# Weight sums and most low parts of the second product by GpSimd alone, and 56 fewer, wider stores of weight blocks

## The chip, the cores and the metric

The kernel runs on one core of one Trainium2 chip. The metric is the device time of one launch in microseconds; the median over runs is what counts. Engines: TensorE (PE, with weight loads as PEld), VectorE (DVE), ScalarE (ACT), GpSimd (POOL), SyncE (SP). Each works through its own queue in order. SP computes nothing here: nearly all DMAs are issued from its queue.

## The reference

An attention over 8 batches of 8 heads (576 positions, 64 wide), heads 0 to 3 with a local mask of 32 positions, heads 4 to 7 with a mask that keeps every 32nd position, followed by a two-layer network on its 4608 x 512 result:

```python
mask_local = (rel >= 0) & (rel < stride)
mask_strided = (rel >= 0) & (pos[None, :] % stride == pos[:, None] % stride)
masks = np.stack([mask_local if h < H // 2 else mask_strided for h in range(H)], axis=0)
scores = np.where(masks[None, :, :, :], scores, -1000000000.0)
...
attn_out = np.matmul(attn, v)
x = np.ascontiguousarray(attn_out.transpose(0, 2, 1, 3)).reshape(B * S, H * D)
h = x @ w_in                                  # [4608,512] @ [512,2048]
g = h * np.clip(h + 3.0, 0.0, 6.0) / 6.0
out = g @ w_out                               # [4608,2048] @ [2048,512]
```

All in float32.

## The kernel before

**Precision.** A float32 product is made of three matmuls of a faster type: high by high, high by low, low by high. Each operand therefore has a high part (a rounding copy by ACT, "hi") and a low part (value minus high part, a subtraction by DVE or POOL, "lo").

**Stages.** Batches 0, 1 and 2 go through both products in a plain way, 512 tokens at a time (`ffn`). From about 345 us on the other five batches go in pairs, (3,4), (5,6) and (7 alone), and use sums of blocks in place of some of the products (a Strassen scheme, 7 products for 8). The pair (3,4) (`super_tile`, about 345 to 545 us) does so in the first product only; the pair (5,6) and batch 7 (`fast_tile`, about 545 to 716 and 716 to 873 us) in both. The attention of later batches is worked in between.

**Weight sums.** The scheme needs sums of weight blocks, split in high and low, in SBUF or in DRAM:

- `combine(g, k)`, eight times while batches 1 and 2 run: of two blocks of w_in it makes two sums of 128x512 (`whole`, L995), four of 128x256 (`sums`, L1003), two high parts (ACT, L1007) and two low parts (`lo`, L1011), and stores them to DRAM (L1018, tiles dS).
- `combine_out(n, slots)`, eight times while the pair (3,4) runs: the same for w_out (`whole` L1144, `sums` L1150, `lo` L1160, stores L1165, tiles dT). Its inputs are the slots `or`, into which blocks of w_out are loaded from DRAM at L1195 (or<-do); the plain second product of this stage reads the same slots.
- `keep_plain` and `keep_block` store the plain blocks (tiles dA, do).

`load_in` (L1105, wr<-dA, wr<-dS) and the loads L1417 (or<-dT) and L1426 (or<-do) in `fast_tile` bring them back.

**First and second product.** Of the first product's seven sums, P, several are gathered by DVE (`added`, L1134) and ACT (`copied`, L1129) into G; the gate is L769 (ACT) and L772 (DVE, G or u from P). L783 and L787 are the high and low parts of the gate for the plain second product (gh on ACT, gl on POOL), L1357 and L1361 (`split`) those of the fast one. `form` makes the first product's operands B (L1058 their low parts, L1064 sums). L526 transposes keys and queries for the attention (kplain, qplain), whose scores are L593. In the fast tiles L1459 adds the second product's cP into C.

**Order.** The program's order is planned when it is built. Every step is given to `op(engine, cost, function, reads, writes, due, ...)`, and `emit` plays the engines through with these costs, choosing what can start soonest, then what is due first. A step that names two engines goes to the one that is free first in this play:

```python
op({"DVE": 1.3, "POOL": 1.45}, 0, whole, reads=[slots[i]], writes=[uk[i]] + ..., due=due)
```

So costs set both the order on each engine and, for such steps, the engine. On the chip an engine runs its queue in that order and waits with whatever stands first.

Of the kernel before, what the change touches and what calls it, by code (L numbers as in the profile page):

```python
# [19 lines left out]
P = 128  # L20
# [9 lines left out]
TOK = 512  # L30
# [143 lines left out]
def attention_ffn(ctx: ExitStack, tc, q, k, v, w_in, w_out, out):  # L174
# [258 lines left out]
    def pair(g):  # L433
# [37 lines left out]
        for x in "qk":  # L471
# [47 lines left out]
            def tr(x=x, nkey=nkey):  # L519
# [6 lines left out]
                nc.vector.transpose(to, tiles[nkey])  # L526
            op("SP", 2.8, load, writes=[nkey], due=due - 35, early=due - 45, after=2.0)
            op("DVE", 0.8 if loc else 1.25, tr, reads=[nkey, "plain"], writes=[tkey[x]], due=due - 18, early=max(due - AHEAD, T0 + OPEN), room=LATE)
# [251 lines left out]
    def split_ops(gk, src, key, du, name, tail=False):  # L780

        def hi():
            nc.scalar.copy(new(xp if gk[0][0] == "x" else gp, gk[0], [P, TOK], F32R, f"gh{name}"), src())  # L783

        def lo():
            to = new(xp if gk[1][0] == "x" else gp, gk[1], [P, TOK], F32R, f"gl{name}")
            (nc.vector if tail else nc.gpsimd).tensor_tensor(out=to, in0=src(), in1=tiles[gk[0]].bitcast(F32), op=ALU.subtract)  # L787
# [157 lines left out]
    for g_ in range(NQ):  # L945
        for nm_ in ("A11", "A12", "S2", "S3", "S1", "A22", "S4"):
            scratch[nm_, g_] = drp.tile([P, 2, 2, SIDE], F32, tag=f"d{nm_}{g_}", name=f"d{nm_}{g_}")
        for nm_ in ("T1", "T2", "T3", "T4"):
            scratch[nm_, g_] = drp.tile([P, 2, 2, SIDE], F32, tag=f"d{nm_}{g_}", name=f"d{nm_}{g_}")
    for fc_ in range(NFC):  # L950
        scratch["o", fc_] = drp.tile([P, 2, TOK], F32, tag=f"do{fc_}", name=f"do{fc_}")

    def keep_block(nm, g, k, due):

        c = (EVEN if nm in ("A11", "S2", "S3") else ODD)[k]
        side = 1 if nm in ("S3", "S1", "A22") else 0
        key = wkey("i", g, c)

        def store():
            nc.sync.dma_start(scratch[nm, g][:, k], tiles[key].bitcast(F32)[:, :, SIDE * side:SIDE * side + SIDE])  # L960
        op("SP", 0.53, store, reads=[key, key + ("lo",)], writes=[("d", nm, g, k)], due=due, early=due - 4.0, after=0.8)

    def keep_plain():
        at = start[1] + 2.0
        step = (start[2] + 10.0 - at) / 24
        for g in range(NQ):
            for nm in ("A11", "A12", "A22"):
                for k in range(2):
                    keep_block(nm, g, k, at)
                    at += step  # L970
        for fc in range(NFC):
            key = wkey("o", fc // FQ, fc % FQ)
            due = start[1] + 20.0 + 6.0 * fc

            def store(fc=fc, key=key):
                nc.sync.dma_start(scratch["o", fc], tiles[key].bitcast(F32))
            op("SP", 0.53, store, reads=[key, key + ("lo",)], writes=[("d", "o", fc)], due=due, early=due - 4.0, after=1.4)

    def combine(g, k, due):
# [12 lines left out]
        for i in range(2):  # L992
            def whole(e, i=i):
                t = tiles[kw[i]].bitcast(F32)
                on(e).tensor_tensor(out=make(i, F32, f"E{g}{k}{i}"), in0=t[:, 0], in1=t[:, 1], op=ALU.add)  # L995
            op({"DVE": 1.2, "POOL": 1.35}, 0, whole, reads=[kw[i], kw[i] + ("lo",)], writes=[keys[i]] + (old(keys[0][:2], 0) if late else []), due=due)
        for n_ in range(4):
            def sums(e, n_=n_):
                u, v_ = temp(0), temp(1)
                u0, u1, v0, v1 = u[:, :SIDE], u[:, SIDE:], v_[:, :SIDE], v_[:, SIDE:]  # L1000
                o, x, y, how = ((v1, u1, v1, ALU.add), (u1, u0, u1, ALU.subtract),
                                (u0, v1, u0, ALU.subtract), (v0, v0, u0, ALU.subtract))[n_]
                on(e).tensor_tensor(out=o, in0=x, in1=y, op=how)  # L1003
# [133 lines left out]
    def combine_out(n, slots, due):  # L1137
# [3 lines left out]
        for i in range(2):  # L1141
            def whole(e, i=i):
                t = tiles[slots[i]].bitcast(F32)
                on(e).tensor_tensor(out=(u, v_)[i](), in0=t[:, 0], in1=t[:, 1], op=ALU.add)  # L1144
            op({"DVE": 1.3, "POOL": 1.45}, 0, whole, reads=[slots[i]], writes=[uk[i]] + (old(("sp", 0), 0) if not n else []), due=due)
        for m in range(4):
            def sums(e, m=m):
                u0, u1, v0, v1 = u()[:, :SIDE], u()[:, SIDE:], v_()[:, :SIDE], v_()[:, SIDE:]
                o, x, y = ((u0, u1, u0), (u1, v1, u1), (v1, v1, u0), (v0, v0, v1))[m]
                on(e).tensor_tensor(out=o, in0=x, in1=y, op=ALU.subtract)  # L1150
            op({"DVE": 0.9, "POOL": 0.85}, 0, sums, writes=uk, due=due + 0.2 + 0.1 * m)
        for i in range(2):
# [8 lines left out]
            op("ACT", 0.63, hi, reads=[uk[i]], writes=[keys[0]] + (old(("sp", 1 + i), 0) if not n else []), due=due + 0.7)  # L1161
            op({"DVE": 1.25, "POOL": 1.4}, 0, lo, reads=[uk[i], keys[0]], writes=[keys[1]], due=due + 0.8)
            for x, nm in enumerate((("T1", "T3"), ("T4", "T2"))[i]):
                def store(i=i, x=x, nm=nm):
                    nc.sync.dma_start(scratch[nm, n // 2][:, n % 2], tiles["sp", 1 + i].bitcast(F32)[:, :, SIDE * x:SIDE * x + SIDE])  # L1165
                op("SP", 0.53, store, reads=keys, writes=[("d", nm, n // 2, n % 2)], due=due + 3.0, after=0.8)

# [119 lines left out]
    def fast_tile(si):  # L1287
# [84 lines left out]
        def second_of(s):  # L1372
# [5 lines left out]
            for j, nm in enumerate(SECONDS):  # L1378
                due = w0 + 2 * j * long
                gks = []  # L1380
                for q in range(2):
# [5 lines left out]
                    if nm == "P6":  # L1387
# [27 lines left out]
                if tn:  # L1415
                    def load(wk=wk, tn=tn):
                        nc.sync.dma_start(home(wk).bitcast(F32), scratch[tn, s].rearrange("p q h d -> p q (h d)"))  # L1417
                    op("SP", 0.53, load, reads=[("d", tn, s, q) for q in range(2)], writes=[wk], due=due - 8.0, early=due - 40.0, after=1.4)
                else:
# [166 lines left out]
```

## Time and profile before

| | |
|---|---|
| median of 3 runs | 881.37 us (880.92 to 884.89) |
| the profiled execution | 884.25 us, of it the span 882.5 us |
| granted TensorE clock, mean | 0.992 of full speed |
| instructions on DVE, POOL, SP | 961, 543 rows busy on DVE and POOL; 598 DMAs or groups of them on SP |
| chain that ended last | PE 79%, POOL 5%, DMA 5%, DVE 4% |
| DMA | 179.12 MB, mean 203 GB/s; HBM written 40.89 MB |

The profile shows one execution. "Busy" is the time in which an engine worked on an instruction; a number in brackets at the end of an instruction's row is how long its engine stood idle before it and what ended that wait. The longest waits of DVE and POOL for one another, and the whole chain, in the page's words:

```profile
PE 79%; POOL 5%; DMA 5%; DVE 4%; issue 3%; ACT 2%; SPq 1%; ACTq 0%; DVEq 0%; POOLq 0%
```

It is to be read as: of the chain that led to the last instruction, four fifths were PE's own work.

### The profile page before, as it was taken

The numbers are of one execution on the slowest core, as the hardware profiler recorded it, in microseconds if no ns is written. First come the engines' busy times: TensorE is split into PE (matmuls) and PEld (weight loads), VectorE is DVE, ScalarE is ACT, GpSimd is POOL, SyncE is SP. The second block draws the span as 40 slices with busy tenths as digits, with TensorE's granted clock in tenths as the row PEclk, the third lists the DMA queues.
The fourth block names the chain that finished last, engine by engine and source line by source line (L and its number), as shares of the span: only waits on it lengthen the run. The fifth ranks groups of instructions, "written<-read, shape, count | busy, mean of one in ns | idle before, by whom it ended". The sixth has DMA issues, their size and how long they took to land.

```text
span 882.5 us, 19109 instructions
## 1 busy us (share of the span) xinstructions
PE 850.9 (96%) x6962; PEld 684.3 (78%) x6962; DVE 605.8 (69%) x961; ACT 558.1 (63%) x1246; POOL 555.3 (63%) x543
## 2 busy tenths in 40 slices
PE   8889999999999999999999799999999999999995
PEld 6667778788888888878778588788888778888884
DVE  5688868565556658683765757377777988777685
ACT  3687656777687876787677476577654645454441
POOL 4678876455547769763574687445865887545472
PEclk9999999999999999999999999999999999999999
DMA  8958713889884466799989697877666658876537
GB/s 218 316 115 230 241 32 76 208 268 246 271 241 104 121 164 196 210 245 245 263 230 266 224 303 213 222 210 207 192 187 192 194 145 250 203 238 191 179 122 141
DMA packets 342252, 179.12 MB, mean 203 GB/s; under 512 B 200784, under 2 KB 322384, under 8 KB 342160
## 3 DMA queue, kind: packets, MB, share of 16 engines
q1 hardware_dynamic: 333764, 176.35, 71.5%
q10 hardware_dynamic: 8396, 1.57, 1.0%
q8 instruction: 55, 0.90, 0.4%
q14 instruction: 37, 0.30, 0.1%
HBM read 136.97 MB, written 40.89 MB: 202 GB/s over the span
## 4 chain that ended last, share of the span: by engine, by line
PE 79%; POOL 5%; DMA 5%; DVE 4%; issue 3%; ACT 2%; SPq 1%; ACTq 0%; DVEq 0%; POOLq 0%
PE P L1122 8%; PE P L1124 7%; PE P L1123 7%; PE ph L848 5%; PE acc L825 5%; PE cP L1443 5%; PE cP L1442 5%; PE cP L1441 5%; PE acc L827 5%; PE ph L849 4%; PE ph L850 4%; PE acc L826 4%; PE acc L1208 3%; PE acc L1210 3%; PE acc L1209 3%
## 5 line engine op out<-in xcount | busy, mean ns | idle before, releaser
L787 POOL TENSOR_TENSOR gl<-u,gh 128x512 fp32r<-128x512 f32 x48 | 65.6, 1368 | 56.2 <-ACT gh L783 40.8
L1459 DVE SCALAR_TENSOR_TENSOR C<-cP,C 128x512 f32<-128x512 f32 x96 | 65.5, 686 | 25.7 <-PE cP L1443 24.9
L1122 PE MATMUL P<-B_T,wr 128*128 128x512 f32 x192 | 76.2, 397 | 3.6 <-ACT G L1129 2.0
L825 PE MATMUL acc<-wo,gh 128*128 128x512 f32 x192 | 77.0, 401 | 0.0
L827 PE MATMUL acc<-wo,gl 128*128 128x512 f32 x192 | 75.3, 392 | 0.3 <-POOL gl L787 0.2
L826 PE MATMUL acc<-wo,gh 128*128 128x512 f32 x192 | 74.9, 390 | 0.0
L1124 PE MATMUL P<-B_T,wr 128*128 128x512 f32 x192 | 74.8, 390 | 0.0
L1123 PE MATMUL P<-B_T,wr 128*128 128x512 f32 x192 | 74.8, 390 | 0.0
L1134 DVE TENSOR_TENSOR G<-P,G 128x512 f32<-128x512 f32 x64 | 43.8, 686 | 42.9 <-PE P L1124 38.3
L1129 ACT COPY G<-P 128x512 f32<-128x512 f32 x64 | 37.6, 587 | 46.5 <-PE P L1124 46.3
L658 POOL TENSOR_TENSOR e<-e,st 96x384 f32<-96x384 f32 (+1 forms) x64 | 47.1, 741 | 19.6 <-DVE st L654 19.3
L693 ACT COPY atloc<-e 32x192 f32<-32x192 f32 x144 | 50.9, 353 | 12.9 <-DVE e L683 11.4
L772 DVE SCALAR_TENSOR_TENSOR u<-u,ph 128x512 f32<-128x512 f32 x48 | 32.8, 686 | 36.3 <-ACT u L769 35.9
L1361 POOL TENSOR_TENSOR sp<-G,sp 128x512 fp32r<-128x512 f32 x26 | 36.0, 1393 | 30.0 <-ACT sp L1357 28.6
L848 PE MATMUL ph<-x,wi 128*128 128x512 f32 x128 | 52.4, 410 | 2.2 <-ACT x L419 1.1
L769 ACT ACTIVATE u<-ph,three 128x512 f32<-128x512 f32 x48 | 33.0, 688 | 31.5 <-PE ph L850 31.2
L849 PE MATMUL ph<-x,wi 128*128 128x512 f32 x128 | 50.7, 396 | 2.3 <-DVE x L422 1.6
L1122 PE MATMUL P<-B_B,wr 128*128 128x512 f32 x120 | 48.0, 400 | 4.9 <-DVE G L1134 3.3
L850 PE MATMUL ph<-x,wi 128*128 128x512 f32 x128 | 50.7, 396 | 0.0
L1123 PE MATMUL P<-B_B,wr 128*128 128x512 f32 x120 | 46.9, 390 | 0.0
L1124 PE MATMUL P<-B_B,wr 128*128 128x512 f32 x120 | 46.8, 390 | 0.0
L1122 PEld LDWEIGHTS P<-B_T,wr 128*128 128x128 f32 x192 | 36.0, 188 | 13.7 <-ACT G L1129 3.3
(619 smaller groups left out, 2673.1 us busy)
## 6 DMA issues: line engine op xcount, KB each, us to landing
wr<-dS SPq DMA_DIRECT2D x96, 256.0 KB
wr<-dA SPq DMA_DIRECT2D x72, 256.0 KB
or<-do SPq DMA_DIRECT2D x32, 512.0 KB
or<-dT SPq DMA_DIRECT2D x32, 512.0 KB
or<-do SPq DMA_DIRECT2D x48, 256.0 KB
rawi<-in_moe_w_in_dram SPq DMA_DIRECT2D x16, 512.0 KB
rawo<-in_moe_w_out_dram SPq DMA_DIRECT2D x16, 512.0 KB
do<-wo SPq DMA_DIRECT2D x16, 512.0 KB
```

Of the source, the lines that this page charges most:

```text
L693: nc.scalar.copy(at[PAD * (a + h):PAD * (a + h) + PAD, :, rows], e[rows, :, PAD * h:PAD * h + PAD])
L787: (nc.vector if tail else nc.gpsimd).tensor_tensor(out=to, in0=src(), in1=tiles[gk[0]].bitcast(F32), op=ALU.subtract)
L825: nc.tensor.matmul(acc, gh, woh, start=fc == 0, stop=False)
L826: nc.tensor.matmul(acc, gh, wol, start=False, stop=False)
L827: nc.tensor.matmul(acc, gl, woh, start=False, stop=end)
L848: nc.tensor.matmul(ph, wih, xh, start=n_ == 0, stop=False)
L849: nc.tensor.matmul(ph, wih, xl, start=False, stop=False)
L850: nc.tensor.matmul(ph, wil, xh, start=False, stop=n_ == NCC - 1)
L1122: nc.tensor.matmul(ph, wh, xh, start=fresh and k == 0, stop=False, skip_group_check=not fresh)
L1123: nc.tensor.matmul(ph, wh, xl, start=False, stop=False, skip_group_check=not fresh)
L1124: nc.tensor.matmul(ph, wl, xh, start=False, stop=k == 1, skip_group_check=not fresh)
L1459: nc.vector.scalar_tensor_tensor(out=tiles[ck], in0=tiles[bank], scalar=1.0 / 6.0, in1=tiles[ck], op0=ALU.mult, op1=ALU.add)
```

## The change

- `whole`, `sums` and `lo` of `combine` and `combine_out` name POOL alone, with costs of 1.3, 0.82 and 1.3.
- The low part in `split` names POOL alone while s is at most 1 in the pair (5,6) and at most 2 in batch 7 (s counts the four groups of the second product); after that it names both engines as before.
- Blocks that were stored side by side go out together: `combine` 32 stores of 256 KB for 64 of 128 KB, `combine_out` 16 of 512 KB for 32 of 256 KB, `keep_plain` 16 of its w_in stores for 24. The bytes stay the same. The DRAM tiles are laid out anew: A1, A2, Su, Sv, Tu, Tv, with `KEPT` saying where each block lies. A store of T is now one run of 4 KB per partition; a load of T (L1417 before) reads four runs of 1 KB per partition where it read one of 4 KB.
- Two planning costs are altered: 3.4 for 2.8 at the loads of queries and keys of batches 5 to 7, 1.3 for 1.35 at L789.

```diff
-    op("SP", 2.8, load, writes=[nkey], due=due - 35, early=due - 45, after=2.0)
+    op("SP", 3.4 if b > 4 else 2.8, load, writes=[nkey], due=due - 35, early=due - 45, after=2.0)
...
-    op("DVE" if tail else "POOL", 0.8 if tail else 1.35, lo, reads=[key, gk[0]], writes=[gk[1]], due=du)
+    op("DVE" if tail else "POOL", 0.8 if tail else 1.3, lo, reads=[key, gk[0]], writes=[gk[1]], due=du)
...
+    KEPT = {"A11": ("A1", 0), "A12": ("A2", 0), "A22": ("A2", 1), "S2": ("Su", 0), "S3": ("Su", 1), "S4": ("Sv", 0), "S1": ("Sv", 1),
+            "T1": ("Tu", 0), "T3": ("Tu", 1), "T4": ("Tv", 0), "T2": ("Tv", 1)}
...
     # combine
-            op({"DVE": 1.2, "POOL": 1.35}, 0, whole, ...)
+            op("POOL", 1.3, partial(whole, "POOL"), ...)
-            op({"DVE": 0.9, "POOL": 0.9}, 0, sums, ...)
+            op("POOL", 0.82, partial(sums, "POOL"), ...)
-            op({"DVE": 1.4, "POOL": 1.4}, 0, lo, ...)
-            for x, nm in enumerate((("S2", "S3"), ("S4", "S1"))[i]):
-                for h in range(2):
-                        nc.sync.dma_start(scratch[nm, g][:, k, h], part.bitcast(F32)[:, SIDE * x:SIDE * x + SIDE])
+            op("POOL", 1.3, partial(lo, "POOL"), ...)
+            for h in range(2):
+                    nc.sync.dma_start(scratch["Su" if i == 0 else "Sv", g][:, k, h], part.bitcast(F32))
...
     # combine_out
-            op({"DVE": 1.3, "POOL": 1.45}, 0, whole, ...)
+            op("POOL", 1.3, partial(whole, "POOL"), ...)
-            op({"DVE": 0.9, "POOL": 0.85}, 0, sums, ...)
+            op("POOL", 0.82, partial(sums, "POOL"), ...)
-            op({"DVE": 1.25, "POOL": 1.4}, 0, lo, ...)
-            for x, nm in enumerate((("T1", "T3"), ("T4", "T2"))[i]):
-                    nc.sync.dma_start(scratch[nm, n // 2][:, n % 2], tiles["sp", 1 + i].bitcast(F32)[:, :, SIDE * x:SIDE * x + SIDE])
-                op("SP", 0.53, store, reads=keys, writes=[("d", nm, n // 2, n % 2)], due=due + 3.0, after=0.8)
+            op("POOL", 1.3, partial(lo, "POOL"), ...)
+                nc.sync.dma_start(scratch[("Tu", "Tv")[i], n // 2][:, n % 2], tiles["sp", 1 + i].bitcast(F32))
+            op("SP", 0.53, store, reads=keys, writes=[("d", ("Tu", "Tv")[i], n // 2, n % 2)], due=due + 3.0, after=1.4)
...
     # split
-            op({"DVE": 1.25, "POOL": 1.4}, 0, lo, reads=[key, gk[0]], writes=[gk[1]], due=du)
+            if both:
+                op({"DVE": 1.25, "POOL": 1.4}, 0, lo, reads=[key, gk[0]], writes=[gk[1]], due=du)
+            else:
+                op("POOL", 1.3, partial(lo, "POOL"), reads=[key, gk[0]], writes=[gk[1]], due=du)
...
     # the loads of T in fast_tile
-                        nc.sync.dma_start(home(wk).bitcast(F32), scratch[tn, s].rearrange("p q h d -> p q (h d)"))
+                        at, x = KEPT[tn]
+                        nc.sync.dma_start(home(wk).bitcast(F32).rearrange("p q (h d) -> p (q h) d", h=2),
+                                          scratch[at, s][:, :, :, SIDE * x:SIDE * x + SIDE].rearrange("p q h d -> p (q h) d"))
```

How many instructions each line has on the two engines, before and after (after's line numbers are a few off; before's are given):

| line | what | DVE | POOL |
|---|---|---|---|
| L995, L1003, L1011 | combine: whole, sums, lo | 6, 13, 8 to 0 | 10, 19, 8 to 16, 32, 16 |
| L1144, L1150, L1160 | combine_out: whole, sums, lo | 6, 10, 4 to 0 | 10, 22, 12 to 16, 32, 16 |
| L1361 | second product's low parts | 41 to 14 | 71 to 98 |
| L1058, L1064 | form: low parts, sums of operands | 18, 9 to 22, 11 | the rest |

(The counts are the program's; the profile lacks a few records and shows fewer.) PE has the same instructions, in another order between about 130 and 530 us. The engines' order is the same up to about 130 us, and nearly the same again from 550 us on.

DVE near the end of the pair (3,4), around the last combine_out (sp are its sums; G_6458, G_6428, u_7c the last gates; qplain and kplain the transposes for the attention), before:

```order
L1150 TENSOR_TENSOR sp_4909<-sp_4909 128x256
L1134 TENSOR_TENSOR G_6458<-P_3_7_6451,G_6458 128x512
L526 STREAM_TRANSPOSE qplain<-qn_3_6244 128x18x4x8
L772 SCALAR_TENSOR_TENSOR G_6458<-u_7b,G_6458 128x512
L772 SCALAR_TENSOR_TENSOR u_7c<-u_7c,P_3_7_6360 128x512
L1134 TENSOR_TENSOR G_6428<-P_3_7_6451,G_6428 128x512
L1160 TENSOR_TENSOR sp_5042<-sp_4909,sp_5042 128x512
L772 SCALAR_TENSOR_TENSOR G_6428<-P_3_7_6451,G_6428 128x512
L683 STREAM_TRANSPOSE e_248<-e_248 96x6x64
L526 STREAM_TRANSPOSE kplain<-kn_3_6310 128x18x4x8
```

and the same place now (the gates are called G_6401, G_6366 and u_7c here, and L1134 is L1133):

```order
L1055 TENSOR_TENSOR B_B_0_3870<-x_10_5435,B_B_0_3870 128x512
L526 STREAM_TRANSPOSE qplain<-qn_3_6177 128x18x4x8
L526 STREAM_TRANSPOSE kplain<-kn_3_6253 128x18x4x8
L1133 TENSOR_TENSOR G_6401<-P_3_7_6390,G_6401 128x512
L1055 TENSOR_TENSOR B_B_1_4466<-x_20_5290,B_B_1_4466 128x512
L1055 TENSOR_TENSOR B_B_1_3979<-x_30_5644,B_B_1_3979 128x512
L772 SCALAR_TENSOR_TENSOR G_6401<-u_7b,G_6401 128x512
L772 SCALAR_TENSOR_TENSOR u_7c<-u_7c,P_3_7_6292 128x512
L1133 TENSOR_TENSOR G_6366<-P_3_7_6390,G_6366 128x512
L1055 TENSOR_TENSOR B_B_0_4496<-x_10_6438,B_B_0_4496 128x512
```

The sums and the low part of combine_out are gone from DVE; in their place stand low parts of the next pair's operands (B_B, `form`), and the transposition of the keys has moved ahead of the gates.

POOL at the same place (gl are the low parts of the gate, L1144 the whole sums from the loaded slots `or`), before:

```order
L1160 TENSOR_TENSOR sp_5042<-sp_4909,sp_5042 128x512
L1144 TENSOR_TENSOR sp_4909<-or_4832 128x512
L1058 TENSOR_TENSOR B_B_0_4447<-x_00_5136,B_B_0_4447 128x512
L1058 TENSOR_TENSOR B_B_0_3909<-x_10_5509,B_B_0_3909 128x512
L787 TENSOR_TENSOR gl_7a<-r_7_6382,gh_7a 128x512
L1150 TENSOR_TENSOR sp_4909<-sp_4909 128x256
L787 TENSOR_TENSOR gl_2e<-G_5196,gh_2e 128x512
```

and now (L1144, L1150 are L1143, L1149):

```order
L1143 TENSOR_TENSOR sp_4839<-or_4811 128x512
L787 TENSOR_TENSOR gl_6c<-u_6c,gh_6c 128x512
L658 TENSOR_TENSOR e_130<-e_130,st_1_6250 96x6x64
L1055 TENSOR_TENSOR B_B_0_4400<-x_00_5063,B_B_0_4400 128x512
L658 TENSOR_TENSOR e_228<-e_228,st_1_6250 96x6x64
L1143 TENSOR_TENSOR sp_4839<-or_4777 128x512
L1149 TENSOR_TENSOR sp_4839<-sp_4839 128x256 x2
L787 TENSOR_TENSOR gl_7a<-r_7_6312,gh_7a 128x512
```

Both whole sums are POOL's now, and the second of them, with two of the narrow sums, still stands ahead of gl_7a.

SP at the same place (or<-do loads w_out for the sums, dT is the store of combine_out), before:

```order
L1105 DMA wr_4659<-dS_121 128x4x128
L1195 DMA or_4832<-do_141 128x1024
L559 DMA vstr<-in_v_dram 18x2x512 x4
L1165 DMA dT_122<-sp_5003 128x2x256
L1165 DMA dT_124<-sp_5003 128x2x256
L1165 DMA dT_125<-sp_5042 128x2x256
L1165 DMA dT_123<-sp_5042 128x2x256
L1195 DMA or_4862<-do_126 128x1024
```

and now:

```order
L1103 DMA wr_4634<-dSv_103 128x4x128
L1163 DMA dTu_104<-sp_4964 128x1024
L1163 DMA dTv_105<-sp_4975 128x1024
L1193 DMA or_4777<-do_121 128x1024
L559 DMA vstr<-in_v_dram 18x2x512 x4
L1193 DMA or_4774<-do_106 128x1024
```

Four stores have become two wider ones, and they stand ahead of the load of the last combine_out's second slot, where they stood behind it.

More of the change, by code (lines that the diff above doesn't have):

```diff
@@ L964, in keep_plain @@
         at = start[1] + 2.0
-        step = (start[2] + 10.0 - at) / 24
+        step = (start[2] + 10.0 - at) / 16
         for g in range(NQ):
-            for nm in ("A11", "A12", "A22"):
+            for nm in ("A1", "A2"):
                 for k in range(2):
@@ L995, in whole @@
                 on(e).tensor_tensor(out=make(i, F32, f"E{g}{k}{i}"), in0=t[:, 0], in1=t[:, 1], op=ALU.add)
-            op({"DVE": 1.2, "POOL": 1.35}, 0, whole, reads=[kw[i], kw[i] + ("lo",)], writes=[keys[i]] + (old(keys[0][:2], 0) if late else []), due=due)
+            op("POOL", 1.3, partial(whole, "POOL"), reads=[kw[i], kw[i] + ("lo",)], writes=[keys[i]] + (old(keys[0][:2], 0) if late else []), due=due)
         for n_ in range(4):
@@ L1003, in sums @@
                 on(e).tensor_tensor(out=o, in0=x, in1=y, op=how)
-            op({"DVE": 0.9, "POOL": 0.9}, 0, sums, writes=keys[:2], due=due + 0.1 * n_)
+            op("POOL", 0.82, partial(sums, "POOL"), writes=keys[:2], due=due + 0.1 * n_)
         for i in range(2):
@@ L1012, in combine, with store @@
             op("ACT", 0.63, hi, reads=[keys[i]], writes=[keys[2]] + (old(keys[2][:2], 0) if late else []), due=due + 0.5)
-            op({"DVE": 1.4, "POOL": 1.4}, 0, lo, reads=[keys[i], keys[2]], writes=[keys[3]], due=due + 0.6)
-            for x, nm in enumerate((("S2", "S3"), ("S4", "S1"))[i]):
-                for h in range(2):
-                    def store(nm=nm, x=x, h=h):
-                        part = home(("S", 1))[:, h] if late else tiles[keys[2 + h]]
-                        nc.sync.dma_start(scratch[nm, g][:, k, h], part.bitcast(F32)[:, SIDE * x:SIDE * x + SIDE])
-                    op("SP", 0.53, store, reads=[keys[2 + h]], writes=[("d", nm, g, k) + ((h,) if h else ())], due=due + 3.0, after=0.8)
+            op("POOL", 1.3, partial(lo, "POOL"), reads=[keys[i], keys[2]], writes=[keys[3]], due=due + 0.6)
+            for h in range(2):
+                def store(i=i, h=h):
+                    part = home(("S", 1))[:, h] if late else tiles[keys[2 + h]]
+                    nc.sync.dma_start(scratch["Su" if i == 0 else "Sv", g][:, k, h], part.bitcast(F32))
+                op("SP", 0.53, store, reads=[keys[2 + h]], writes=[("d", "Su" if i == 0 else "Sv", g, k) + ((h,) if h else ())], due=due + 3.0, after=0.8)
     def form(si):
@@ L1144, in whole @@
                 on(e).tensor_tensor(out=(u, v_)[i](), in0=t[:, 0], in1=t[:, 1], op=ALU.add)
-            op({"DVE": 1.3, "POOL": 1.45}, 0, whole, reads=[slots[i]], writes=[uk[i]] + (old(("sp", 0), 0) if not n else []), due=due)
+            op("POOL", 1.3, partial(whole, "POOL"), reads=[slots[i]], writes=[uk[i]] + (old(("sp", 0), 0) if not n else []), due=due)
         for m in range(4):
@@ L1150, in sums @@
                 on(e).tensor_tensor(out=o, in0=x, in1=y, op=ALU.subtract)
-            op({"DVE": 0.9, "POOL": 0.85}, 0, sums, writes=uk, due=due + 0.2 + 0.1 * m)
+            op("POOL", 0.82, partial(sums, "POOL"), writes=uk, due=due + 0.2 + 0.1 * m)
         for i in range(2):
@@ L1348, in fast_tile, with split @@
         ring = sets()
-        def split(gk, src, key, du, name):
+        def split(gk, src, key, du, name, both):
             def make(x):
@@ L1416, in load @@
                     def load(wk=wk, tn=tn):
[L1417 to L1418 removed]
+                        at, x = KEPT[tn]
+                        nc.sync.dma_start(home(wk).bitcast(F32).rearrange("p q (h d) -> p (q h) d", h=2),
+                                          scratch[at, s][:, :, :, SIDE * x:SIDE * x + SIDE].rearrange("p q h d -> p (q h) d"))
+                    op("SP", 0.53, load, reads=[("d", KEPT[tn][0], s, q) for q in range(2)], writes=[wk], due=due - 8.0, early=due - 40.0, after=1.4)
                 else:
```

26 lines of the change are left out of this document (12 added, 14 removed).

## The prediction

> **What bounds the kernel now.** I read the page's busy line first, then the windows (columns: stretch, its length, busy PE, PEld, DVE, ACT, POOL, granted clock, DMA share, GB/s), then the rows of PE that had to wait.
>
> ```profile
> PE 850.9 (96%) x6962; PEld 684.3 (78%) x6962; DVE 605.8 (69%) x961; ACT 558.1 (63%) x1246; POOL 555.3 (63%) x543
> 145.00:335.00 190.00, 189.90 (x1831) 153.38 (x1830) 113.55 (x206) 142.94 (x383) 114.11 (x134) 1.00 0.70 195
> 340.00:500.00 160.00, 155.08 (x1197) 124.50 (x1189) 105.36 (x165) 112.18 (x270) 98.72 (x105) 0.99 0.86 241
> 716.00:862.00 146.00, 145.94 (x641) 119.93 (x640) 109.92 (x147) 70.49 (x117) 84.88 (x60) 1.00 0.67 193
> ```
>
> TensorE (PE) is the bound: 850.9 of 882.5 us, and it runs without a gap from 145 to 335 and from 716 to 862. The change takes nothing from PE. It can gain only where PE stands still, and relieving DVE (69%) or SP is worth nothing elsewhere. The order of the instructions is unchanged up to about 130 us. So every wait of PE after 135 us is looked at; those over half a microsecond are:
>
> ```profile
> 422.50 0.50 PE L1122 MATMUL P<-B_B,wr 128*128 128x512 f32 x1 [1.00 <-DVE u_3c L772]
> 426.15 0.50 PE L1122 MATMUL P<-B_B,wr 128*128 128x512 f32 x1 [0.63 <-DVE G L772]
> 491.46 0.50 PE L1122 MATMUL P<-B_B,wr 128*128 128x512 f32 x1 [3.29 <-DVE G L1134]
> 504.26 1.14 PE L593 MATMUL ps<-kplain,qplain 64*64 64x36 f32 x64 [2.69 <-DVE kplain L526]
> 566.90 0.50 PE L1122 MATMUL P<-B_T,wr 128*128 128x512 f32 x1 [0.68 <-ACT G L1129]
> 703.73 0.50 PE L1122 MATMUL P<-B_T,wr 128*128 128x512 f32 x1 [0.68 <-ACT G L1129]
> 713.75 0.50 PE L1122 MATMUL P<-B_T,wr 128*128 128x512 f32 x1 [1.58 <-DVE G L1134]
> ```
>
> The number in brackets is the wait. The last three lie in the fast tiles, where the order of DVE and POOL hardly changes; they stay. The first four lie in the stage of the first pair of batches, where combine_out runs. What DVE and POOL did ahead of the first two:
>
> ```profile
> 417.29 1.29 POOL L1144 TENSOR_TENSOR sp<-or 128x512 f32<-128x512 f32 x1 [4.78 <-DMA or<-do]
> 419.31 1.94 DVE L1150 TENSOR_TENSOR sp<-sp 128x256 f32<-128x256 f32 x2 [3.81 <-POOL sp L1150]
> 421.77 0.68 DVE L772 SCALAR_TENSOR_TENSOR u_3c<-u_3c,P 128x512 f32<-128x512 f32 x1
> 424.31 1.18 DVE L1144 TENSOR_TENSOR sp<-or 128x512 f32<-128x512 f32 x1
> ```
>
> This is place A. DVE runs in order. Its weight sums stood idle 3.81 us for POOL's, which stood 4.78 us for a load of w_out, and the gate that PE needed was queued behind them; then a sum of 1.18 us stood before the next gate. Place B, seventy microseconds on:
>
> ```profile
> 479.72 0.57 SPq L1195 DMA_DIRECT2D or<-do  x1
> 486.60 1.29 POOL L1144 TENSOR_TENSOR sp<-or 128x512 f32<-128x512 f32 x1 [6.82 <-DMA or<-do]
> 487.93 1.47 DVE L1150 TENSOR_TENSOR sp<-sp 128x256 f32<-128x256 f32 x1 [4.90 <-POOL sp L1144]
> 489.81 0.99 DVE L1150 TENSOR_TENSOR sp<-sp 128x256 f32<-128x256 f32 x1
> 490.73 0.68 DVE L1134 TENSOR_TENSOR G<-P,G 128x512 f32<-128x512 f32 x1
> 490.48 1.45 POOL L787 TENSOR_TENSOR gl_7a<-r,gh_7a 128x512 fp32r<-128x512 f32 x1
> 480.00:500.00 20.00, 16.71 (x67) 13.28 (x66) 14.71 (x16) 10.31 (x21) 13.40 (x11) 0.91 0.77 237
> ```
>
> The load, issued at 479.72, held POOL 6.82 us, and through it DVE 4.90, and through that PE 3.29. The granted clock of this slice is 0.91 where its neighbours have 1.00. So the gap costs more than its 3.29: 0.09 × 20 us = 1.8. By the Trainium skill (TensorE: Matmul & The Clock Gate, "What's actually happening") a window of about 3.4 us without work halves the clock; the granted clock here agrees. Place C is different:
>
> ```profile
> 495.08 1.28 POOL L1160 TENSOR_TENSOR sp<-sp,sp 128x512 fp32r<-128x512 f32 x1
> 495.56 6.36 DVE L1160 TENSOR_TENSOR sp<-sp,sp 128x512 fp32r<-128x512 f32 x1
> 500.08 1.28 POOL L787 TENSOR_TENSOR gl_0e<-G,gh_0e 128x512 fp32r<-128x512 f32 x1
> 502.93 1.19 DVE L526 STREAM_TRANSPOSE kplain<-kn 128x576 f32<-128x576 f32 x1
> L1160 DVE TENSOR_TENSOR sp<-sp,sp x4: 693/1950/6355, 394.8 to 495.6; 128x512 fp32r<-128x512 f32 x4
> ```
>
> (The last row gives minimum/mean/maximum ns.) A subtraction that takes 0.69 us at best took 6.36, from 495.56 to 501.92, just while POOL worked through its run from 495.08 to 501.36. The keys' transposition behind it was late, and PE waited 2.69.
>
> **The change part by part.** Weight sums and low parts in combine_out, POOL alone: 6 + 10 + 4 instructions leave DVE. All of A, B and C had one of them in front of the late operation, so 1.00 + 0.63 + 3.29 + 1.8 + 2.69 = 9.4 us can go. What is late next at A and B is POOL, which still waits for the loads; its queue holds gl_7a, and P's operand, behind the sums. What it costs there:
>
> ```profile
> L1144 POOL TENSOR_TENSOR sp<-or x10: 1289/1292/1576, 352.6 to 486.6; 128x512 f32<-128x512 f32 x10
> L1150 POOL TENSOR_TENSOR sp<-sp x22: 727/741/1198, 355.1 to 491.9; 128x256 f32<-128x256 f32 x22
> L1160 POOL TENSOR_TENSOR sp<-sp,sp x12: 1281/1294/1297, 361.9 to 495.1; 128x512 fp32r<-128x512 f32 x12
> POOL sp L1144 <- DMA or<-do: 21.8, 6, 6.8
> 80.00:100.00 20.00, 19.68 (x113) 15.20 (x111) 18.19 (x33) 15.00 (x28) 18.51 (x17) 1.00 0.67 229
> ```
>
> POOL gets 6 × 1.292 + 10 × 0.741 + 4 × 1.294 = 20.3 us. With the 98.7 busy and the 21.8 in which it stands for loads (fourth row: total, times, longest), that makes 141 of 160 us, 88%. From 80 to 100 POOL was at 18.51 of 20, 93%, and PE at 19.68: such a load alone does not stop PE. So I cost it at nothing, except at B. There, in the new order, the loads' successor on SP changes: the two 512 KB stores of the step before, which wait for POOL's low parts, stand ahead of the load of or_4777, and POOL's second whole sum waits for that load ahead of gl_7a. A lateness between 0 and the old 3.29 us is left for PE; I take 1.5, the middle, since the old load took 6.9 us from its issue to POOL's start and the new one has no better place.
>
> Sums and low parts in combine, POOL alone: 6 + 13 + 8 leave DVE. By the rows of the same shapes POOL gains 6 × 1.292 + 13 × 0.741 + 8 × 1.294 = 27.7 on 114.1 in the 190 us from 145 to 335: 142, 75%. PE stands 0.1 us there: no gain, and the cover is 48 us of free POOL time. Were it gone, PE would wait for gl (L787) as in the row at 490.48.
>
> Low parts of the second product: 27 leave DVE, 27 × 1.296 (row below) = 35 us for POOL over the last two tiles. From 716 to 862 half of that makes 84.9 + 17.5 = 102 of 146. PE has 0.06 us of idle time there: nothing to gain, and nothing lost while POOL keeps 40 us free. A split on POOL instead of DVE takes 1.296 for 1.200, so its matmul is no later than 0.1 us.
>
> ```profile
> L1361 POOL TENSOR_TENSOR sp<-G,sp x26: 1281/1296/1746, 569.7 to 862.5; 128x512 fp32r<-128x512 f32 x26
> L1361 DVE TENSOR_TENSOR sp<-G,sp x14: 650/1200/1776, 589.2 to 846.3; 128x512 fp32r<-128x512 f32 x14
> L1165 SPq DMA_DIRECT2D dT<-sp x32: 359/534/1431, 368.0 to 502.3; - x32
> L1417 SPq DMA_DIRECT2D or<-dT x32: 325/326/1602, 556.8 to 866.8; - x32
> L1426 SPq DMA_DIRECT2D or<-do x48: 517/518/1739, 547.2 to 856.5; - x48
> 870.51 0.47 PE L1441 MATMUL cP<-B_B,or 128*128 128x512 f32 x1 [0.41 <-DMA or<-dT]
> ```
>
> Stores: 56 fewer on SP, at about 0.53 us each (third row) 30 us of SP's time. SP is no bound, PE waits for none of these loads outside the last one, and the bytes are the same: nothing, with a bound of +1 us where a wider store at C's place holds SP longer. Its gain, the loads behind the stores coming earlier, is inside the four gaps.
>
> Loads of T (or<-dT) now read four runs of 1 KB per partition in place of one of 4 KB. Issuing goes from 0.326 towards the 0.518 that the row of w_out's loads shows, 32 × 0.19 = 6 us of SP, hidden by the lead that the loads have, except for the last one, which PE waits for at 870.51: +0.2 of issue, and as much again or twice that for four times the packets. Bounds 0 and +1.6 (SP's worst row); I take +0.6.
>
> Altered costs of the key loads and of L789: they change only the order, from about 130 us on. PE's order moves there too, so a new gap of the size of the old ones is possible anywhere from 130 to 530; this is in the range.
>
> The sum: 884.25 (the profiled execution: span 882.5 and 1.75 around it) − 9.4 + 1.5 + 0.6 = 877.0. The median of the runs, 881.37, is 2.9 below the profiled execution; the gaps have to do with when loads land and may be smaller in a median run, so half of this difference goes off: 875.5.
>
> By the Trainium skill (SBUF — State Buffer, "Who interferes with whom") a DVE instruction with two SBUF inputs and a GpSimd instruction that reads SBUF lock each other out, the later one waiting until the first has ended. By it C would have cost about one POOL instruction, 1.3 us, and the sum would be 2.69 less favourable in the worst case, 879.7; the 6.36 us over five POOL instructions speaks for a longer exclusion.
>
> **The rivals.** First: POOL takes DVE's place as the late engine. The 21.8 us in six waits for w_out's loads speak for it, and that gl_7a and two operands of the first product stay behind them; against it that the gates on DVE are no longer behind. Gap B then comes back whole, 3.29 + 1.8 less the 1.5 counted, +3.6 on 875.5: 879.1, no change that can be told. C may come back in the same way: four operands (L1058, two SBUF inputs) stand on DVE there in the new order.
>
> Second, the side of a loss: POOL becomes the bound from 340 to 505. It has 160 − 141 = 19 us free by the sum above. Each of the eight steps now waits on POOL for both loads; if each waits 4 us more, 32 us, the free time is overdrawn by 13, and PE is later by that: 875.5 + 13 = 888.5. It decides when the waits exceed 41 us, twice the 21.8. Against it: the loads may be issued earlier with fewer stores before them.
>
> Third: the split runs make T's loads late in the fast tiles. 16 loads a tile × 0.4 = 6.4 us per tile on top of a DMA share of 0.67: if half of them in one tile showed, 3.2 us, 878.7. For it only the 0.41 at 870.51; against it the lead.
>
> That nothing happens is possible too: if the gaps shown belong to the profiled execution alone, the median moves by less than 2 us.
>
> **How the numbers follow.** This kernel's measurement can tell about 0.5%, 4.4 us: faster is below 877.0, slower above 885.8. My forecast (A, B mostly and C gone) has 0.55. POOL in DVE's place, 0.22, T's loads 0.05 and nothing 0.07 all end within 0.5%, but a fifth of the first comes out below 877. POOL as the bound: 0.11. So faster 0.60, same 0.29, slower 0.11. The range goes from 869.5 (all four gaps gone, full difference to the median: 884.25 − 9.4 − 2.9 = 872, and some 2.5 us less for other waits of PE that shrink) to 882.5 (rival one together with rival three's 3.2). The likeliest is 875.5.
>
> **What the profile of the changed kernel would show.** Right: no wait of PE over 1 us between 340 and 510 that ends with DVE; the slice at 480 to 500 at clock 1.00; POOL busy 119 of those 160 us. POOL over 142 and still PE at 189.9 from 145 to 335. Wrong: PE's waits ending with POOL's gl (L787) or with B_B from POOL; POOL's wait for or<-do well above 22 us in sum; a DVE row of over 3 us beside POOL's; more than 1 us at the last or<-dT; new gaps between 130 and 335.

## The result and the profile after

The changed kernel takes 878.16 us in the median of 22 runs, the kernel before 882.73 in 22 runs beside it: ratio 0.9949, 95% interval 0.9934 to 0.9964. That is 4.6 us, just at the 0.5% that the prediction set as its line. The profiled execution took 878.14 us, its span 876.4.

The busy line, and windows of the changed kernel (columns as before: stretch, length, PE, PEld, DVE, ACT, POOL, clock, DMA share, GB/s):

```profile
PE 851.4 (97%) x6962; PEld 683.9 (78%) x6962; DVE 541.0 (62%) x896; ACT 558.3 (64%) x1247; POOL 614.5 (70%) x607
145.00:335.00 190.00, 190.00 (x1829) 153.23 (x1828) 91.88 (x179) 143.69 (x380) 133.27 (x158) 1.00 0.68 192
340.00:500.00 160.00, 156.77 (x1278) 126.14 (x1277) 86.38 (x153) 117.68 (x289) 114.84 (x126) 0.99 0.92 246
400.00:420.00 20.00, 18.14 (x158) 14.59 (x157) 7.95 (x17) 14.06 (x35) 13.91 (x20) 0.91 0.93 249
480.00:500.00 20.00, 19.77 (x166) 15.46 (x165) 13.79 (x20) 16.30 (x40) 16.13 (x18) 1.00 0.75 204
```

The work went over as told: DVE 605.8 to 541.0 us, POOL 555.3 to 614.5, PE unchanged. The slice at 480 has its full clock again; another one, at 400, has lost it. PE's waits over 0.4 us after 125 us:

```profile
129.00 0.50 PE L848 MATMUL ph<-x,wi 128*128 128x512 f32 x1 [0.82 <-DVE u L772]
403.61 1.25 PE L593 MATMUL ps<-kplain,qplain 64*64 64x36 f32 x64 [1.86 <-ACT x L419]
458.83 0.50 PE L1121 MATMUL P<-B_B,wr 128*128 128x512 f32 x1 [0.66 <-DVE G L772]
477.08 0.50 PE L1121 MATMUL P<-B_B,wr 128*128 128x512 f32 x1 [0.48 <-DVE G L772]
...
566.88 0.50 PE L1121 MATMUL P<-B_T,wr 128*128 128x512 f32 x1 [1.25 <-ACT G L1128]
...
707.36 0.50 PE L1121 MATMUL P<-B_T,wr 128*128 128x512 f32 x1 [1.58 <-DVE G L1133]
864.80 0.47 PE L1444 MATMUL cP<-B_B,or 128*128 128x512 f32 x1 [1.09 <-DMA or<-dTv]
```

The four gaps of before are gone or small, and a new one of 1.86 us stands at 403.61. Its history, on POOL and ACT:

```profile
396.86 1.28 POOL L1143 TENSOR_TENSOR sp<-or 128x512 f32<-128x512 f32 x1 [7.25 <-DMA or<-do]
400.83 0.62 ACT L1155 CAST sp<-sp 128x512 fp32r<-128x512 f32 x1 [4.22 <-POOL sp L1149]
402.45 0.62 ACT L1155 CAST sp<-sp 128x512 fp32r<-128x512 f32 x1 [1.00 <-POOL sp L1149]
402.98 0.58 ACT L419 COPY x<-pv 128x512 f32<-128x512 f32 x1
```

It is the old chain with another victim. POOL waits 7.25 us for a load of w_out; ACT, with the high parts of the sums at the head of its queue, waits 4.22 and 1.00 for POOL; behind them stands a copy of the attention's, and PE waits for that. The clock of this slice is 0.91, so the gap costs about 1.8 us more than its length.

How much of the gain lies where is read between two marks that all these kernels have: PE's wait for u (0.82 us, at 129.00 here) and its second wait for ACT's G in the first fast tile (at 566.88 here). In the kernel before these are:

```profile
132.31 0.50 PE L848 MATMUL ph<-x,wi 128*128 128x512 f32 x1 [0.82 <-DVE u L772]
573.31 0.50 PE L1122 MATMUL P<-B_T,wr 128*128 128x512 f32 x1 [0.68 <-ACT G L1129]
```

From mark to mark 441.0 us before and 437.9 after: 3.1 us of the 6.1 between the two profiled executions. Ahead of the first mark, where the order is unchanged, the changed kernel is 3.3 us earlier. That part is no effect of the change that these profiles can show: the first mark lies between 128.6 and 133.4 us in all fourteen profiles, at 133.4 in a kernel as fast as this one. Behind the second mark it is 0.3 us slower.

### The profile page after: what moved, and what is told of

Read it like the earlier page. It is cut to its first block, busy times and chain, and to the rows that moved or that the text cites. A ratio compares the mean times of both kernels' runs of the same rounds, so it can differ in the third digit from the quotient of the medians.

```text
span 876.4 us, 19018 instructions
## 1 busy us (share of the span) xinstructions
PE 851.4 (97%) x6962; PEld 683.9 (78%) x6962; DVE 541.0 (62%) x896; ACT 558.3 (64%) x1247; POOL 614.5 (70%) x607
## 4 chain that ended last, share of the span: by engine, by line
PE 77%; POOL 7%; DMA 7%; DVE 4%; ACT 2%; issue 2%; SPq 0%; ACTq 0%; POOLq 0%
PE P L1121 8%; PE P L1122 7%; PE P L1123 7%; PE cP L1444 5%; PE cP L1445 5%; PE cP L1446 5%; PE acc L825 5%; PE ph L848 4%; PE acc L827 4%; PE acc L826 4%; PE ph L850 4%; PE ph L849 4%; PE acc L1206 3%; PE acc L1208 3%; PE acc L1207 3%; DMA rawo<-in_moe_w_out_dram 2%
## 5 line engine op out<-in xcount | busy, mean ns | idle before, releaser
L787 POOL TENSOR_TENSOR gl<-u,gh 128x512 fp32r<-128x512 f32 x48 | 65.2, 1360 | 30.1 <-issue 15.3
L1133 DVE TENSOR_TENSOR G<-P,G 128x512 f32<-128x512 f32 x64 | 43.9, 688 | 60.3 <-PE P L1123 47.1
L1359 POOL TENSOR_TENSOR sp<-G,sp 128x512 fp32r<-128x512 f32 x34 | 47.1, 1399 | 24.0 <-ACT sp L1355 24.0
L658 POOL TENSOR_TENSOR e<-e,st 128x144 f32<-128x144 f32 (+1 forms) x64 | 44.4, 696 | 19.4 <-DVE st L654 16.6
```

## The experiments

Each was timed beside the kernel before on the same chip, in 12 runs (e5 in 6, e7 in 8, the change in 22). The kernel before had medians of 881.63 us beside e1 to e4, 881.41 beside e5 to e8 and 881.06 beside e9 to e12. The ratio is worked out over the runs of both and is not quite the ratio of the medians. "Stretch" is the time between the two marks in the one profile of each.

| | what | median us | ratio, 95% interval | stretch us |
|---|---|---|---|---|
| | before | | | 441.0 |
| | the change | 878.16 | 0.9949, 0.9934 to 0.9964 | 437.9 |
| e1 | combine_out on POOL alone | 880.80 | 0.9990, 0.9972 to 1.0009 | 440.0 |
| e2 | stores alone, new order | 877.63 | 0.9973, 0.9950 to 0.9995 | 439.8 |
| e3 | all but combine_out | 877.80 | 0.9964, 0.9939 to 0.9989 | 435.8 |
| e4 | combine_out on POOL, old order | 880.87 | 1.0002, 0.9982 to 1.0023 | 440.4 |
| e5 | the change, T stored as before | 876.91 | 0.9951, 0.9933 to 0.9969 | 437.4 |
| e6 | stores alone, old order | 879.88 | 0.9985, 0.9970 to 1.0000 | 439.3 |
| e7 | both planning costs alone | 876.71 | 0.9945, 0.9924 to 0.9966 | 436.2 |
| e8 | the whole work, old order | 882.25 | 1.0018, 0.9997 to 1.0039 | 440.6 |
| e9 | load cost 3.4 alone | 876.88 | 0.9949, 0.9931 to 0.9966 | 435.7 |
| e10 | L789's cost 1.3 alone | 880.57 | 0.9989, 0.9973 to 1.0004 | 441.7 |
| e11 | the change, costs as before | 879.86 | 0.9978, 0.9956 to 0.9999 | 435.8 |
| e12 | an unrelated cost nudged | 881.07 | 0.9988, 0.9967 to 1.0008 | 442.2 |

**Parts of the work: e1 to e4.**

```diff
 e1, in the kernel before, combine_out's three steps
-op({"DVE": 1.3, "POOL": 1.45}, 0, whole, ...)   # and sums, lo
+op("POOL", 1.3, partial(whole, "POOL"), ...)
 e2: the changed kernel with every {"DVE": ..., "POOL": ...} and both costs of before: the stores alone
 e3: the changed kernel with combine_out's three steps on {"DVE": ..., "POOL": ...} again
 e4, in the kernel before, inside combine_out; the plan is left alone
-on(e).tensor_tensor(out=(u, v_)[i](), ...)      # and sums, lo
+nc.gpsimd.tensor_tensor(out=(u, v_)[i](), ...)
```

> The kernel before with one part of the change: combine_out's whole sums, narrow sums and low parts planned for POOL alone. Theory 1 (the gain comes from these steps leaving DVE's queue): most of the 4.6 us, so 877 to 880 against 882.7, and no wait of PE over 1 us that ends with DVE between 340 and 510 us. Rival 2 (the gain comes from fewer and wider stores, which let SP issue the loads of w_out earlier): no gain, 882 to 884. Rival 3 (the gain lies in the unchanged first 130 us and in chance): 882 to 884, with the first matmul of batch 2's first product (L848 at 132.3 before, 129.0 after) anywhere between.

> The kernel before with the other half alone: stores widened and scratch laid out anew, all engines as before. Theory 1: no gain; the last load of T is later by 0.7 us (0.41 before, 1.09 after), so 882.5 to 884. Rival 2: 878 to 880, and POOL's wait for or<-do below the 21.8 us of before.

> The changed kernel with combine_out's steps given back to whichever engine is free, the rest of the change kept. Theory 1: the gain is lost, 881 to 884, with waits of PE on DVE between 340 and 510 us of 3 us or more in sum. Rival 2: 877 to 880.

> The kernel before in its own order, the queue of PE unchanged to the row; the 20 steps of combine_out that stood on DVE are carried out by POOL at the same place of the program. Theory 1 (DVE's blocked queue is the cause of gaps A, B and C): the waits of 1.00, 0.63, 3.29 and 2.69 us go, 875 to 879. The first rival of the prediction (POOL late in DVE's place): the waits return on POOL or ACT at the same places, 880 to 884. Rival 3 (chance): 882 to 884.

The theory that the gain comes from freeing DVE's queue fell in three kernels: the part that frees it gives 0.1% with an interval across 1 (e1), nothing in the old order (e4), and without this part most of the gain stays (e3, 0.9964). In e4, where PE's queue is that of before row for row, the waits on DVE at places A, B and C did go, but those at B and C came back on POOL, and a new one on DVE stands at 453.74 (the last two rows are windows, columns as above):

```profile
453.74 0.50 PE L1122 MATMUL P<-B_B,wr 128*128 128x512 f32 x1 [1.14 <-DVE u_5c L772]
489.43 0.50 PE L1210 MATMUL acc<-or,gl_7a 128*128 128x512 f32 x1 [2.15 <-POOL gl_7a L787]
496.66 0.50 PE L1123 MATMUL P<-B_B,wr 128*128 128x512 f32 x1 [2.16 <-POOL B_B L1058]
480.00:500.00 20.00, 15.70 (x56) 11.66 (x55) 6.81 (x8) 9.73 (x22) 17.38 (x16) 0.86 0.76 241
500.00:520.00 20.00, 20.00 (x193) 15.91 (x193) 5.62 (x12) 15.59 (x38) 13.84 (x17) 0.97 0.95 267
```

2.15 and 2.16 us where 3.29 and 2.69 had stood: the three waits sum to 5.5 us for the 7.6 of before. The clock takes most of that back. It is 0.86 and 0.97 in these two slices where it was 0.91 and 1.00, by the working above 3.4 us for 1.8, so that the stretch is only 0.6 us shorter. It is the first rival of the prediction, gl_7a and all. In e1 the planner makes an order of its own and PE has waits of 3.48, 0.31 and 1.85 us between 465 and 500; nothing is won by it either.

e2 stood against this with 877.63, but its interval reaches to 0.9995, and e2 has also another order. So order and work had to be parted.

**Work and order parted: e5 to e8.**

```diff
 e6, in the kernel before; the plan is left alone: of two stores that belong together the first goes out wide, the second is dropped
+if (at, n) not in stored:
+    stored.add((at, n))
+    nc.sync.dma_start(scratch[at, n // 2][:, n % 2], tiles["sp", 1 + i].bitcast(F32))
 e8: e6, and on(e) is POOL in combine, combine_out and split's first groups, as in e4
 e7, in the kernel before, nothing else
-op("SP", 2.8, load, writes=[nkey], ...)
+op("SP", 3.4 if b > 4 else 2.8, load, writes=[nkey], ...)
-op("DVE" if tail else "POOL", 0.8 if tail else 1.35, lo, ...)
+op("DVE" if tail else "POOL", 0.8 if tail else 1.3, lo, ...)
 e5: the changed kernel with T1 to T4 apart in DRAM, stored 128x2x256 and loaded in runs of 4 KB as before
```

> The kernel before with the stores alone widened and the scratch laid out anew, in the order of before: the queues of PE, ACT, DVE and POOL are the same to the row, and on SP a wide store stands where the first of the narrow ones stood. The stores with a new order (e2) gave 878.6 in the mean against 881.8. Theory A (fewer stores leave SP free, and loads of w_out come earlier): as much here, 877.5 to 880, and POOL's wait for or<-do well below 21.8 us. Theory B (the gain is in the order that the planner made after the change of the stores): nothing here, 881 to 883.

> The whole change in the order of before: as the stores above, and the weight sums, their low parts and the low parts of the second product's first groups carried out by POOL wherever before's plan had them on DVE. PE's and ACT's queues are the same to the row. Theory A: 877 to 879.5. Theory B: 880.5 to 883, since the engine alone gave 0.2 us in before's order.

> The kernel before with the two planning costs alone altered (3.4 for 2.8 at the loads of keys and queries of batches 5 to 7, 1.3 for 1.35 at L789): no instruction is added, removed or moved to another engine but by the plan, and the order moves. Theory A: 881 to 883. Theory B in its strong form (these two costs make the better order): 877.5 to 880; in its weak form (any new order draws a new set of gaps): anything from 878 to 885.

> The changed kernel with the sums of w_out stored and loaded as before: 32 stores of 256 KB in place of 16 of 512 KB, and each load of T one run of 4 KB per partition. If the split runs cost what the prediction said (0.6 us at the last load, 0.41 before and 1.09 after), that wait goes back to 0.4 us and the time to 877.5 or 0.7 us below the changed kernel's; if the 16 fewer stores in the stage of the pair (3,4) are the gain (theory A), 880 to 882.

This is the turn of the study. The whole of the work, in the old order, gives no gain: 1.0018, interval 0.9997 to 1.0039. The two planning costs, with no work altered, give all of it: 0.9945. Theory A, that fewer stores are the cause, is left with 0.15% at the most likely (e6, 0.9985, an interval that ends at 1.0000). Its mechanism is there, a total of 14.2 us of POOL's waits for w_out's loads in e6 (six waits, the longest 4.5) where before had 21.8, and place B shrinks to 0.91; place C stays whole (3.43, shown further below):

```profile
POOL sp L1150 <- DMA or<-do: 14.2, 6, 4.5
484.79 0.50 PE L1128 MATMUL P<-B_B,wr 128*128 128x512 f32 x1 [0.91 <-DVE G L1140]
```

e8's profile shows where the work's own effect goes, B and C on POOL once more, and C larger (L1064 here is L1058 of before, the low parts of operands):

```profile
489.91 0.50 PE L1219 MATMUL acc<-or,gl_7a 128*128 128x512 f32 x1 [2.01 <-POOL gl_7a L787]
497.14 0.80 PE L1129 MATMUL P<-B_B,wr 128*128 128x512 f32 x1 [3.76 <-POOL B_B L1064]
```

e5 leaves the question of T's loads open: with the old layout the last wait is 0.64 us there, with the new one 1.09 in the changed kernel, and the ratios (0.9951 and 0.9949) are the same. All fourteen profiles together lean towards a cost: with the old layout six of eight show no wait of PE for these loads (0.41 and 0.64 in the others), with the new one two of six (0.49, 0.71, 0.72 and 1.09 in the others). It is too small to be told in the times.

```profile
864.09 0.47 PE L1445 MATMUL cP<-B_B,or 128*128 128x512 f32 x1 [0.64 <-DMA or<-dT]
```

**Which cost, or any new order: e9 to e12.**

```diff
 e9, in the kernel before
-op("SP", 2.8, load, writes=[nkey], ...)
+op("SP", 3.4 if b > 4 else 2.8, load, writes=[nkey], ...)
 e10, in the kernel before: L789's 1.35 to 1.3
 e11, in the changed kernel: 3.4 back to 2.8, 1.3 back to 1.35
 e12, in the kernel before, split_ops
-op("ACT", 0.63, hi, reads=[key], ...)
+op("ACT", 0.64, hi, reads=[key], ...)
```

> The kernel before with one number altered, the planning cost of the loads of keys and queries of batches 5 to 7, 3.4 for 2.8. No work is altered. Theory B1 (the plan had these loads too short, and the true cost sets the loads of w_out and the transpositions in a better order): nearly all of the 4.9 us that both costs gave, 876.5 to 878.5 against 881.5. Theory B2 (any new order draws a new set of waits, and the order of before is a poor draw): anywhere from 876 to 883, and no better than the nudge. Theory B3 (the cost at L789 does it): 881 to 882.5.

> The kernel before with the other number alone, 1.3 for 1.35 as the planning cost of POOL's low parts of the gate at L789. No work is altered. Theory B1: 881 to 882.5. Theory B2: 876 to 883. Theory B3: 876.5 to 878.5.

> The changed kernel with the two planning costs as before (2.8 and 1.35): all of the work that the change speaks of, none of its costs for other steps. If the gain hangs on these two numbers (B1 or B3): 880 to 883. If any new order will do (B2): 876 to 883, the likeliest 878 to 880, as for the stores with a new order (878.6 in the mean).

> The kernel before with a number that has nothing to do with the change: the planning cost of ACT's high parts of the gate, 0.64 for 0.63. The order of all engines moves from about 340 us on (402 of PE's rows in a comparison of the two, for 896 with both costs). B1 and B3: no gain, 881 to 882.5. B2: a draw like the others, 876 to 883; a value under 879.5 speaks for a poor order of before, one over 880.5 against it.

One number does it. The loads' cost of 3.4 for 2.8 gives 0.9949 by itself, as the whole change does. The other cost and the nudge, which move the order no less, give 0.9989 and 0.9988, intervals across 1. The five kernels that have the 3.4 (the change, e3, e5, e7, e9) lie at 0.9945 to 0.9964, the eight without it at 0.9973 to 1.0018. So "any new order will do" (B2) is not what happened, though not dead. Of the eight, three keep the order of before (e4, e6, e8: 0.9985 to 1.0018), and the five with a new order (e1, e2, e10, e11, e12) all lie below 1, at 0.9973 to 0.9990. Part of the 0.51% may therefore be what other orders bring too. e11's single profile has a stretch as short as e9's.

Where e9 gains is seen in its marks and the waits between them:

```profile
133.37 0.51 PE L848 MATMUL ph<-x,wi 128*128 128x512 f32 x1 [0.82 <-DVE u L772]
442.39 0.50 PE L1122 MATMUL P<-B_T,wr 128*128 128x512 f32 x1 [0.45 <-ACT r L1129]
479.14 0.50 PE L1122 MATMUL P<-B_B,wr 128*128 128x512 f32 x1 [1.21 <-DVE G L772]
484.39 0.50 PE L1122 MATMUL P<-B_T,wr 128*128 128x512 f32 x1 [0.19 <-ACT G L1129]
488.30 0.50 PE L1122 MATMUL P<-B_T,wr 128*128 128x512 f32 x1 [2.25 <-DVE r L772]
...
569.02 0.50 PE L1122 MATMUL P<-B_T,wr 128*128 128x512 f32 x1 [0.67 <-ACT G L1129]
```

435.7 us from mark to mark, 5.3 less than before: its four waits sum to 4.1 for 7.6, and 1.8 is the clock, which is 1.00 in e9 throughout this stretch. So the gain does sit in the gaps at A, B and C, as forecast. But it is order, not the move off DVE, that took them: DVE still carries 20 of combine_out's 64 instructions here, as many as before. What is left at 488.30 is the chain of place B, with a sum on DVE that waits for POOL and the gate behind it:

```profile
486.62 1.02 DVE L1150 TENSOR_TENSOR sp<-sp 128x256 f32<-128x256 f32 x1 [4.19 <-POOL sp L1150]
```

Why this cost matters was looked for on SP. Each group of four loads of queries (qn) or keys (kn) is planned at 2.8 us. Two of the groups of the kernel before in the stage of the pair (3,4), with start and duration:

```profile
379.68 3.68 SPq L350 DMA_DIRECT2D qn<-in_q_dram  x4
403.39 5.22 SPq L350 DMA_DIRECT2D qn<-in_q_dram  x4
```

The twelve groups there between 358 and 479 us take 41.2 us of SP, 3.43 each, where the plan has 33.6. So the plan has the loads of w_out behind these groups, and the sums that wait for them, too early. That 3.4 is the true cost does not follow, for in e9 the same twelve groups take 33.7 us, 2.81 each, the old cost; in the other twelve profiles the mean lies between 2.95 and 3.83. The counterparts of the two groups in e9:

```profile
380.16 2.54 SPq L350 DMA_DIRECT2D qn<-in_q_dram  x4
401.28 2.29 SPq L350 DMA_DIRECT2D qn<-in_q_dram  x4
```

What the longer cost did for certain is another order. DVE's queue at place A, in the program's order, before:

```
L1134 TENSOR_TENSOR G_5605<-P_3_3_5637,G_5605 128x512
L1150 TENSOR_TENSOR sp_4909<-sp_4909 128x256 x2
L772 SCALAR_TENSOR_TENSOR G_5605<-u_3b,G_5605 128x512
L772 SCALAR_TENSOR_TENSOR u_3c<-u_3c,P_3_3_5513 128x512
```

and in e9, as the trace shows it (the two gates come at 418.72 and 419.33, and the same two sums behind the whole group of gates):

```profile
418.72 0.69 DVE L772 SCALAR_TENSOR_TENSOR G<-u_3b,G 128x512 f32<-128x512 f32 x1 [2.30 <-ACT u_3b L769]
419.33 0.68 DVE L772 SCALAR_TENSOR_TENSOR u_3c<-u_3c,P 128x512 f32<-128x512 f32 x1
...
422.38 0.65 DVE L772 SCALAR_TENSOR_TENSOR G<-P,G 128x512 f32<-128x512 f32 x1
423.88 1.96 DVE L1150 TENSOR_TENSOR sp<-sp 128x256 f32<-128x256 f32 x2 [0.85 <-POOL sp L1150]
```

With the longer cost the plan puts the sums of the late load behind the gates that PE needs; they are still DVE's, they wait 0.85 us for POOL, and PE, at 20.00 of 20 us from 400 to 440, does not notice. At place C the keys' transposition (L526) stands ahead of the last gates and of combine_out's low part, where it stood behind them. That this is why 3.4 is better is read from these two kernels; no third value of the cost was tried, and with the five new orders above it stays open how much of it another order could have had by luck.

## Why the prediction was right or wrong

The time (875.5 forecast, range 869.5 to 882.5, measured 878.16) and the sign were right. The reason was wrong, so the hit is luck: the term that carries the forecast brought nothing by itself (e4, e8), and a term put at nothing brought as much as the whole change. Nearly all the signs of being right came as well (no wait of PE over 1 us on DVE between 340 and 510, the clock at 1.00 from 480, POOL at 114.84 us for 119, PE at 190.00 of 190); they could not tell the new order from the moved work.

- **What bounds, and where a gain can lie.** Right. PE runs through the other stages as before (190.00 of 190 us from 145 to 335), and what moved between the two marks lies in PE's waits between 340 and 510 and in the clock there.
- **"All of A, B and C had one of them in front of the late operation, so ... 9.4 us can go."** This is the step that failed. Taking the DVE instruction out of the chain does not shorten it, since its root at A and B, a late load of w_out, stays, and at C operands late on POOL took the place of the late keys: e4 1.0002, e1 0.9990. The prediction had the first rival's mechanism in full (gl_7a and operands behind POOL's wait) and gave it 0.22. It left out ACT: the high parts L1156 wait for POOL's sums, and ACT's copies for the attention stand behind them.
- **"Altered costs ... they change only the order."** The second failure, and the dearer one: a term costed at nothing was worth 0.51%, some 4.5 us (e9), the whole of the result. The row that could have raised the question is that of the loads L350: the plan says 2.8, the trace of before 3.43 in this stage. The prediction compared no planned cost with its measured one.
- **Stores.** Nothing forecast; 0.15% measured in the old order, with an interval that touches none. Not settled.
- **Sums of combine and split's low parts.** Nothing forecast for PE, and next to nothing seen: 190.00 of 190 in the changed kernel, with POOL at 133.27 us where 142 was forecast, and in e3 and e8 no wait of PE that ends with them. Only e11 has one wait of PE for POOL in that stretch, 0.43 us for gl (L787) at 252.09, the kind that the prediction named should POOL's free time run out.
- **T's loads.** +0.6 forecast; the last wait rose from 0.41 to 1.09 in the profiled executions, with anything from none to 0.72 for the same layout elsewhere. A cost of this size is likely but not shown.
- **Rival two, POOL as the bound.** Did not come: POOL 114.84 of 160 where 119 was forecast, and its wait for or<-do 22.8 us, far from the 41 that it needed.

## What to carry to other kernels

When an engine's instruction is late because of what it waits for, moving it to another engine moves the victim; follow the chain to its root (here a transfer that SP issued late) before a gap is booked as a gain. Where a planner orders the program, its costs are part of the change: set each altered cost beside the duration in the trace, in the stage in question, remember that this duration is no constant (3.43 us before, 2.81 in e9), and try the costs alone. And to learn what a change of work does, hold the order fixed: the same work gave 0.9949 with its new order and costs and 1.0018 in the old order.

## What the runs showed of the hardware

A DVE instruction with two SBUF inputs can be held up for as long as POOL works without a pause. In e6 the low part of combine_out (0.69 us alone) took 6.36 us again, to the digit as before; in e5 two low parts of operands took 9.96, the first alone 8.29, while POOL went from 488.56 to 498.15 with gaps under 0.1 us, and PE's wait for them was 2.88:

```profile
488.89 6.36 DVE L1166 TENSOR_TENSOR sp<-sp,sp 128x512 fp32r<-128x512 f32 x1
497.59 1.94 PE L593 MATMUL ps<-kplain,qplain 64*64 64x36 f32 x64 [3.43 <-DVE kplain L526]
```

```profile
488.74 9.96 DVE L1057 TENSOR_TENSOR B_B<-x,B_B 128x512 fp32r<-128x512 f32 x2
488.56 1.28 POOL L787 TENSOR_TENSOR gl_2e<-G,gh_2e 128x512 fp32r<-128x512 f32 x1
496.54 1.61 POOL L787 TENSOR_TENSOR gl_1e<-G,gh_1e 128x512 fp32r<-128x512 f32 x1
498.75 0.50 PE L1124 MATMUL P<-B_B,wr 128*128 128x512 f32 x1 [2.88 <-DVE B_B L1057]
```

The Trainium skill (SBUF — State Buffer, "Who interferes with whom") lets the later of two such instructions wait until the first has ended, which would be one POOL instruction, 1.3 us; the runs show a wait through five and more in a row. That it is this lock was not tried by itself.

The clock fell after a short wait: 1.86 us at 403.61 in the changed kernel, followed by 1.2 us of small score matmuls; the stretch from 404 to 408 had 0.63 of it. Longer waits left it whole: 2.69 us at place C before (second row) and 2.25 us at 488.30 in e9 (third row). So the length of the wait alone does not decide here.

```profile
404.00:408.00 4.00, 4.00 (x66) 3.29 (x59) 0.90 (x2) 3.35 (x11) 3.76 (x4) 0.63 1.07 357
500.00:520.00 20.00, 17.31 (x171) 13.60 (x172) 8.41 (x14) 15.09 (x38) 11.28 (x15) 1.00 0.93 257
480.00:500.00 20.00, 17.55 (x156) 13.60 (x155) 14.34 (x19) 15.80 (x39) 14.10 (x14) 1.00 0.76 228
```

The Trainium skill (TensorE: Matmul & The Clock Gate, "Why this matters for your kernels") warns of gaps above some 3 us; here a shorter one, with thin work behind it, cost about 1.8 us more, by estimate (0.09 of 20 us at the slice's 0.91).
